# Two-layer transformer kernel on one core: VectorE's share of the softmax exponentials as E + E(1+f)(1+f)/2 from 16-bit patterns

## The chip, the core and the metric

The kernel runs on one core of a Trainium2 chip. TensorE (PE) multiplies matrices into PSUM; its weight loads (PEld) are shown apart. ScalarE (ACT) evaluates functions such as exp, VectorE (DVE) does elementwise work on SBUF and PSUM, GpSimd (POOL) does elementwise work on SBUF alone, and SyncE (SP) issues the DMAs. Each engine takes its instructions in program order and waits on semaphores for the others. The metric is the device time of one launch in microseconds, as the median over repeated runs; lower is better.

## The reference

Two layers with the same weights, 2048 tokens, width 448, 16 heads of 28, hidden width 1792, all in bf16. Each layer is an attention block and an MLP with squared ReLU, both behind a layer norm and with a residual.

```python
def _A_ref(x, wqkv, wo):                      # H = 16, Dh = 28
    qkv = (x @ wqkv).reshape(B, S, 3, H, Dh).transpose(2, 0, 3, 1, 4)
    q, k, v = qkv[0], qkv[1], qkv[2]
    p = softmax(einsum("bhqd,bhkd->bhqk", q, k) * Dh ** -0.5)
    o = einsum("bhqk,bhkd->bhqd", p, v)
    return o.transpose(0, 2, 1, 3).reshape(B, S, D) @ wo
def _B_ref(x, w1, b1, w2, b2):
    h = relu(einsum("bsd,df->bsf", x, w1) + b1)
    return einsum("bsf,fd->bsd", h * h, w2) + b2
x = x + _A_ref(_layernorm(x), A_wqkv, A_wo)
x = x + _B_ref(_layernorm(x), B_w1, B_b1, B_w2, B_b2)
x = x + _A_ref(_layernorm(x), A_wqkv, A_wo)
x = x + _B_ref(_layernorm(x), B_w1, B_b1, B_w2, B_b2)
```

The softmax needs 16 x 2048 x 2048 exponentials in each layer. The kernel takes exp without subtracting the row's maximum, sums the exponentials by extra columns of ones in V, and divides at the end.

## The kernel before

**Units, groups, passes.** The attention of a layer is cut into passes (one query block of 256 or 128 rows, four heads, a range of key blocks) and a pass into units: one head, 512 scores for each of 128 partitions. There are 2048 units. A group takes three units: TensorE writes their transposed scores into the three banks of one PSUM tile `sc` (L1061, four row tiles of 32 so that heads run beside each other), of which there are two. ScalarE then turns a group's scores into bf16 exponentials in an SBUF tile `pt` (L1087), 1536 columns wide if all three units are its own, 1024 wide if the third was given to VectorE. There are 683 groups and twelve `pt` buffers. When enough key blocks of a pass have their exponentials, TensorE multiplies them by V into the pass's PSUM tile `oT` (L1284, four column tiles of 32). Projections, layer norms and the MLP of other query blocks are worked into the same stream (L769 for their matmuls).

**A unit on VectorE.** The queries are scaled so that a score is a power of two in fixed point (`FRAC` = 17 fraction bits). VectorE reads the scores from PSUM, adds a constant and limits them from below (`take`, L1148) into 32-bit integers in one of the rooms `R_v` (`v_y`, or parts of K and V that are free). Their halves are a fraction and an exponent. `line` (L1177) makes a linear function of the fraction in fp16, `power` (L1191) makes a power of two, E, from the exponent as a bf16 pattern; both may run on GpSimd or VectorE. `square` (L1194) squares the line's result on VectorE and `close` (L1200) multiplies it by E. The exponential is E + a·a·E. Where a buffer is free for it, E stays and is multiplied by V on its own, as a second product in the same TensorE operation (`twice`); else `one` (L1197) adds 1 before the closing product. The result stands in the third part of the group's own `pt`, or, if the unit belongs to a later pass, in a cell `R_pd` (tile `pd`, or free parts of V, K, or the hidden tiles).

**The planner.** The order of all instructions is made in Python before the launch. Streams (`s_stream` scores, `e_stream` ScalarE's exponentials, `p_stream` value matmuls, `a_unit`/`a_rest` for units on VectorE, the chains of the MLP) offer their next operation with a cost and the resources that it takes and frees; `Planner.run` takes the one that can start first, with priorities, and holds back a TensorE operation that would make the next scores late. Operations marked `port` on VectorE and GpSimd take turns. `apart` decides whether a group's third unit goes to VectorE: by VectorE's load over the last `SPAN` us against `BUSY` or, when the MLP work is `behind`, against `LOW`, and by its backlog against `TB`/`TB2`. `PACE` holds parameter values that apply from a group's number on; `FORCE` and `SKIP` list groups in which `apart` answers yes or no without asking for the load.

Of the kernel before, what the change touches and what calls it, by code (L numbers as in the profile page):

```python
# [55 lines left out]
L0E = 1280  # L56
L0N = 4.8
L1E = 1900
L1N = 5.6
# [79 lines left out]
FORCE = (17, 47, 84, 107, 111, 144, 215, 237, 240, 241, 271, 322, 341, 347, 354, 363, 368, 379, 404, 413, 423, 428,  # L139
         434, 438, 440, 453, 457, 472, 495, 512, 515, 532, 561, 608, 614, 628, 633, 640, 641, 648, 652, 667)  # L140
SKIP = (20, 38, 46, 66, 190, 202, 227, 235, 246, 299, 302, 357, 362, 384, 461, 465, 474, 475, 489, 504, 520, 542,
        607, 649, 650)
PACE = {
    0: {'BUSY': 1.05, 'LOW': 1.0, 'CHUNK': 2, 'EV': 2.9, 'FAR': 6, 'KEEP': 2, 'L1N': 5.2, 'LAG': 3, 'LEAD': 18,
         'MARGIN': -1, 'MORE': 1, 'PRE': 0.5, 'SLACK': 0.7, 'SPAN': 11, 'TB': 1.6, 'TB2': 0.9, 'V_AGE': 6, 'V_LAST':
         3, 'V_PAST': 2, 'C_PRIO': 1.6, 'V_PRIO': 8.5, 'V_LATE': 3.5, 'V_WAIT': 5, 'EPRIO': 6, 'ASIDE': 2.0,
         'SPARE': 1, 'VSPARE': 2, 'NEAR': 3, 'SOON': 0.3, 'VGAP': 0.03, 'PWAIT': 1, 'PNEAR': 0.2, 'PORTP': 0.0},
    8: {'V_PAST': 5, 'LEAD': 12},
    16: {'SPAN': 8, 'EPRIO': 4, 'SPARE': 3, 'PRE': 0.8},
    24: {'V_AGE': 2},  # L150
    32: {'V_AGE': 8},
    40: {'MORE': 3, 'V_LAST': 2.5},
    48: {'MORE': 1, 'TB2': 3.0},
    56: {'VSPARE': 1},
    64: {'TB': 2.0, 'PNEAR': 0.15, 'MARGIN': 1.5},
    72: {'KEEP': 6},
    88: {'PWAIT': 4, 'TB2': 0.6, 'C_PRIO': 1.2},
    96: {'EV': 1.3},
    104: {'EPRIO': 6, 'V_PAST': 0, 'CHUNK': 3},
    120: {'V_LAST': 3, 'PWAIT': 1, 'SPARE': 1, 'L1N': 5.6},  # L160
    128: {'TB': 4.2},
    136: {'TB': 2.2, 'V_AGE': 3},
    144: {'TB': 1.6, 'V_LAST': 2.2, 'V_LATE': 4.6, 'PWAIT': 4},
    152: {'V_AGE': 5},
    176: {'EV': 2.2},
    184: {'V_LAST': 3, 'SPARE': 0},
    240: {'SPAN': 15, 'LOW': 0.8},
    248: {'V_PAST': 2, 'PORTP': 1},
    272: {'SPARE': 3},
    280: {'MARGIN': -3, 'SPARE': 1},  # L170
    288: {'VGAP': 0, 'NEAR': 9},
    296: {'SPARE': 0, 'SOON': 0.6},
    312: {'V_AGE': 6},
    320: {'PWAIT': 0.6},
# [12 lines left out]
    440: {'V_LATE': 2.6, 'V_LAST': 3},
    456: {'MARGIN': 0.5, 'LOW': 0.9, 'V_PRIO': 4},
    464: {'PRE': 0.5},
    496: {'L1N': 5.0},  # L190
    512: {'VSPARE': 3, 'KEEP': 4, 'V_LAST': 2.2},
    520: {'BUSY': 1.02, 'ASIDE': 0},
    528: {'V_AGE': 5, 'V_WAIT': 2},
    536: {'EV': 1.5, 'VSPARE': 1, 'SPAN': 8},
    552: {'V_AGE': 2, 'C_PRIO': 1.6},
    560: {'V_LAST': 3, 'PORTP': 1},
    608: {'L1N': 5.6},
    616: {'L1N': 5.8, 'LAG': 12, 'V_LATE': 3.5, 'SPARE': 2},
    624: {'VSPARE': 20},
    632: {'ASIDE': 0.5},  # L200
    640: {'SPARE': 3},
    648: {'V_LAST': 2.5},
    664: {'CHUNK': 2, 'L1N': 5.0},
# [29 lines left out]
LAT = {"PE": 0.25, "ACT": 0.3, "DVE": 0.07, "POOL": 0.10, "DMA": 2.0, "-": 0.0}  # L233
# [5 lines left out]
class Planner:  # L239
# [3 lines left out]
    def __init__(self):  # L243
        self.clock = {"PE": 0.0, "ACT": 0.0, "DVE": 0.0, "POOL": 0.0, "DMA": 0.0, "-": 0.0}
# [53 lines left out]
    def run(self):  # L298
        while self.streams:
# [61 lines left out]
            self.clock[e] = o.end - (OVER if e == "DVE" and o.dur > 0.1 else 0.0) + (PGAP if e == "POOL" else 0.0)  # L361
# [22 lines left out]
def kernel(  # L384
# [556 lines left out]

    def apart(i, now, us, soon=SOON):
# [4 lines left out]
        if sum(r.when() is not None and r.when() <= now + soon for r in sets_of(units[i])) <= (0 if soon else pending[0]):  # L947
            return None
# [640 lines left out]
```

## Time and profile before

| | |
|---|---|
| median of 3 runs | 817.91 us (817.5 to 819.25) |
| profiled execution | 821.79 us, of which the span is 817.4 us |
| TensorE clock granted | 0.996 |
| TensorE busy | 783.8 us (96%), 12133 matmuls |
| VectorE busy | 768.5 us (94%), 1784 instructions |
| ScalarE busy | 801.3 us (98%), 700 instructions |
| GpSimd busy | 422.9 us (52%), 678 instructions |
| DMA | 17.99 MB, mean 22 GB/s; 255 GB/s in the first 20 us |

Each row of the page's table of costly groups reads: line of the kernel, engine, operation, output tile <- input tiles, shapes, count | busy time in us, mean ns of one | idle time of the engine just before these instructions, and what ended most of it. Busy time counts overlapping instructions of the group once. Rows of a timeline give the start in us, the duration in us and the count. Rows by stretches give, after the bounds, the busy us of PE, PEld, DVE, ACT and POOL with the number of instructions, the granted clock, and the DMA's share and GB/s.

### The profile page before, as it was taken

Reading aid. Unit: us, or ns where it says so; the run is one execution under the profiler, and the core shown is the slowest. Engines: PE = TensorE matmul, PEld = TensorE weight load, DVE = VectorE, ACT = ScalarE, POOL = GpSimd, SP = SyncE. Lnnn points to the kernel's source line nnn. Section 1 sums busy time; section 2 is a strip of 40 time slices with the busy share of each in tenths; the row PEclk is TensorE's granted clock in tenths of the full one; section 3 lists DMA queues with packets and bytes.
Section 4 is the critical chain, followed back from the end, with each engine's and each line's share of the span. In section 5 each row is a group of like instructions: output and inputs, shape, how many; then the busy total and the mean of one; then the engine's idle time right before and its main releaser. Section 6 shows DMA issues by size and latency. Waiting matters only on the chain.

```text
span 817.4 us, 28983 instructions
## 1 busy us (share of the span) xinstructions
PE 783.8 (96%) x12133; PEld 427.8 (52%) x12133; DVE 768.5 (94%) x1784; ACT 801.3 (98%) x700; POOL 422.9 (52%) x678
## 2 busy tenths in 40 slices
PE   8999999999999999999999999879999999999998
PEld 4555554554554555555455545445454545545666
DVE  8999999999999999999999999999999999999954
ACT  8999999999999999999999999999999999999994
POOL 3356756566556466554555566665556455412400
PEclk9999999999999999999999999989999999999999
DMA  9200010000000000000000000011000000000000
GB/s 255 73 3 2 15 28 18 16 17 16 16 3 15 16 16 16 15 4 15 2 2 3 2 3 2 16 29 29 24 20 21 21 27 15 28 14 15 22 14 13
DMA packets 32318, 17.99 MB, mean 22 GB/s; under 512 B 17786, under 2 KB 31739, under 8 KB 32188
## 3 DMA queue, kind: packets, MB, share of 16 engines
q1 hardware_dynamic: 32188, 16.16, 7.1%
q8 instruction: 94, 1.54, 0.8%
q14 instruction: 36, 0.29, 0.1%
HBM read 13.87 MB, written 2.06 MB: 19 GB/s over the span
## 4 chain that ended last, share of the span: by engine, by line
PE 69%; ACT 16%; DVE 10%; issue 3%; DMA 1%; POOL 0%; ACTq 0%; SPq 0%; DVEq 0%
PE mt L769 29%; PE sc L1061 22%; PE oT L1284 16%; ACT pt L1087 16%; PE tp L672 2%; DVE v_y L1148 1%; DVE r L1480 1%; DVE st L619 1%; DVE pt L1200 1%; PE sc L769 1%; DVE K_sb L1148 1%; DVE K_sb L792 1%; DMA rec<-scr 1%; DVE pt L1194 1%; DVE xn L732 0%
## 5 line engine op out<-in xcount | busy, mean ns | idle before, releaser
L1087 ACT ACTIVATE pt<-sc 128x1536 bf16<-128x1536 f32 (+1 forms) x683 | 789.8, 1337 | 3.9 <-PE sc L1061 3.4
L1061 PE MATMUL sc<-Q_sb,K_sb 32*128 32x256 bf16 (+1 forms) x4712 | 283.0, 266 | 27.7 <-ACT pt L1087 24.4
L1061 PEld LDWEIGHTS <-K_sb 32*128 32x128 bf16 x4712 | 103.1, 92 | 199.8 <-issue 135.7
L1284 PEld LDWEIGHTS <-V_sb 128*32 128x32 bf16 x4922 | 127.9, 96 | 47.4 <-issue 40.6
L1284 PE MATMUL oT<-pt,V_sb 128*32 128x256 bf16 (+1 forms) x4196 | 151.6, 269 | 0.0
L1177 POOL TENSOR_SCALAR pt<-v_y 128x512 f16<-128x512 uint16 x121 | 78.5, 648 | 98.9 <-DVE v_y L1148 29.7
L769 PE MATMUL mt<-xnT,w 128*128 128x256 bf16 (+1 forms) x896 | 118.7, 271 | 0.0
L1148 DVE TENSOR_SCALAR v_y<-sc 128x512 int32<-128x512 f32 x163 | 110.5, 680 | 2.4 <-PE sc L1061 1.8
L1194 DVE TENSOR_TENSOR pt<-pt 128x512 f16<-128x512 f16 x234 | 96.4, 423 | 3.4 <-POOL pt L1177 3.3
L769 PEld LDWEIGHTS <-w 128*128 128x128 bf16 x952 | 78.0, 98 | 34.4 <-issue 26.2
L1480 DVE TENSOR_SCALAR r<-mt 128x512 bf16<-128x512 f32 x108 | 73.1, 677 | 2.1 <-PE mt L769 1.7
L769 PE MATMUL mt<-w,V_sb 128*128 128x448 bf16 (+1 forms) x288 | 68.9, 348 | 0.0
L1191 POOL TENSOR_SCALAR v_y<-v_y 128x512 int16<-128x512 int16 x70 | 45.5, 650 | 30.6 <-DVE pt L1194 9.3
L1148 DVE TENSOR_SCALAR K_sb<-sc 128x512 int32<-128x512 f32 x81 | 55.0, 680 | 1.6 <-PE sc L1061 1.4
L1177 POOL TENSOR_SCALAR pt<-K_sb 128x512 f16<-128x512 uint16 x56 | 36.4, 651 | 33.9 <-DVE K_sb L1148 15.0
L1420 DVE TENSOR_TENSOR x_sb<-x_sb,mt 128x448 bf16<-128x448 bf16 (+1 forms) x62 | 37.5, 604 | 9.4 <-PE mt L769 9.0
L1177 POOL TENSOR_SCALAR pt<-V_sb 128x512 f16<-128x512 uint16 x45 | 30.2, 671 | 24.3 <-DVE V_sb L1148 7.8
L1148 DVE TENSOR_SCALAR V_sb<-sc 128x512 int32<-128x512 f32 x61 | 41.5, 680 | 1.2 <-PE sc L1061 0.9
L1200 DVE TENSOR_TENSOR pt<-pt,K_sb 128x512 bf16<-128x512 f16 x92 | 39.8, 433 | 0.3
L619 DVE BATCH_NORM_STATS2 st<-x_sb 128x6 f32<-128x448 bf16 x62 | 37.9, 613 | 0.7 <-DMA x_sb<-in_A_x_dram 0.4
L769 PEld LDWEIGHTS <-V_sb 128*128 128x128 bf16 x302 | 24.9, 98 | 25.0 <-issue 11.2
L1284 PE MATMUL oT<-K_sb,V_sb 128*32 128x256 bf16 x214 | 34.1, 274 | 0.0
(157 smaller groups left out, 1048.9 us busy)
## 6 DMA issues: line engine op xcount, KB each, us to landing
rec<-scr SPq DMA_DIRECT2D x54, 128.0 KB
x_sb<-in_A_x_dram SPq DMA_DIRECT2D x8, 224.0 KB
out_dram<-x_sb SPq DMA_DIRECT2D x15, 112.0 KB
w<-in_B_w_dram SPq DMA_DIRECT2D x1, 1568.0 KB
w<-in_B_w_dram SPq DMA_DIRECT2D x1, 1344.0 KB
dn<-oT_sb SPq DMA_DIRECT2D x54, 4.0 KB
V_sb<-in_A_wqkv_dram SPq DMA_DIRECT2D x4, 168.0 KB
scr<-dn SPq DMA_DIRECT2D x27, 8.0 KB
```

The source lines that it names most:

```text
L619: nc.vector.bn_stats(out=box["st"][:, :], in_=x_sb[:, t0 + j, :] if src is None else src())
L769: nc.tensor.matmul(box["t"][:, c0:c0 + n], lhsT=lhsT() if callable(lhsT) else lhsT, rhs=rhs, start=a, stop=b)
L1061: nc.tensor.matmul(dst[k][:, i * nt * P:(i + 1) * nt * P], lhsT=K_sb[l][rows, g, (kb + i) * P:(kb + i + 1) * P], rhs=Q_sb[rows, g, t0 * P: ...
L1087: t = nc.scalar.activation(out=pt[:, 0:n], in_=gbuf[gi]["sc"][:, 0:n], func=AF.Exp, scale=float(np.log(2.0)) * 2.0 ** -FRAC)
L1148: t = nc.vector.tensor_scalar(out=y, in0=src, scalar1=EXP_BIAS, scalar2=EXP_LOW, op0=ALU.add, op1=ALU.max)
L1177: on(e).tensor_scalar(out=box["a"], in0=box["f"], scalar1=EXP_LINE[0], scalar2=EXP_LINE[1], op0=ALU.add, op1=ALU.mult)
L1191: on(e).tensor_scalar(out=box["e"].bitcast(DT.int16), in0=box["n"], scalar1=64.0, scalar2=EXP_BASE, op0=ALU.mult, op1=ALU.add)
L1194: nc.vector.tensor_tensor(out=box["a"], in0=box["a"], in1=box["a"], op=ALU.mult)
L1200: nc.vector.tensor_tensor(out=box["pd"], in0=box["aa"], in1=box["e"], op=ALU.mult)
L1284: nc.tensor.matmul(box["t"][DHP * hh:DHP * hh + DHP, 0:n], lhsT=V_sb[l][:, tb, 4 * g + hh, :], rhs=p, start=begin and j < G, stop=close an ...
L1420: nc.vector.tensor_tensor(out=x_sb[:, tb, lo:hi], in0=x_sb[:, tb, lo:hi], in1=t[:, 0:hi - lo], op=ALU.add)
L1480: nc.vector.tensor_scalar(out=r[:, 0:w], in0=t[:, 0:w], scalar1=0.0, scalar2=None, op0=ALU.max)
```

## The change

A score now has 7 fraction bits, so that adding a constant and rounding to a 16-bit integer gives the pattern of a bf16 number z = E(1+f), E a power of two and f the fraction of the mantissa. A unit on VectorE takes these steps, with line numbers of the changed kernel:

- `take` (L1124): scores from PSUM plus a constant, limited from below, as int16 patterns z. They go straight into the third part of the group's `pt`, or into a cell for a later pass.
- `whole` (L1146): E. On GpSimd, z - 63.5 + 1.5·2^30, which rounds to whole powers of two and leaves E's pattern in the low half of each 32-bit word, in a room `R_v`. On VectorE it would be a mask; the order has all 309 on GpSimd.
- `half` (L1150): mask and set of bits on VectorE, which give (1+f)/2 as bf16, in a cell.
- `close` (L1154): z times that, in place: E(1+f)(1+f)/2.

The exponential is E + E(1+f)(1+f)/2, of which E is always a product with V of its own. These products are TensorE operations of their own (L1221), collected over heads (`XMIN`), between the pass's other value matmuls (L1257). A new stream `t_stream` takes the `pt` buffer when the scores are there, since VectorE may be the first to write it. `room_for` and `cell_for` keep some rooms and cells for the oldest pass. `apart` asks for free cells rather than rooms and prefers a head that has had few such units. `behind` compares with a table of progress (`TRACK`). `FORCE` and `SKIP` become empty, and of the parameter table only the set at group 0 remains, with other values.

```diff
-FRAC = 17
-EXP_BIAS = -0.03899196872583688 * 2.0 ** FRAC
-EXP_LOW = -56.0 * 2.0 ** FRAC
-EXP_BASE = 126.0 * 2.0 ** 7 + 27.0
-EXP_LINE = (2.40163417 * 2.0 ** 16, 0.34787667 * 2.0 ** -16)
+FRAC = 7
+EXP_MEAN = 0.58627
+EXP_BASE = (127.0 - EXP_MEAN) * 2.0 ** FRAC
+WHOLE = 1.5 * 2.0 ** 30
+EXP_LOW = 160.0
...
+ADUR = 0.29
+LADD = 0.15
+HDUR = 0.30
+RES = 2
+RES2 = 4
+XMIN = 4
...
-FORCE = (17, 47, 84, 107, 111, 144, 215, 237, 240, 241, 271, 322, 341, 347, 354, 363, 368, 379, 404, 413, 423, 428,
...
-SKIP = (20, 38, 46, 66, 190, 202, 227, 235, 246, 299, 302, 357, 362, 384, 461, 465, 474, 475, 489, 504, 520, 542,
...
+FORCE = ()
+SKIP = ()
 PACE = {
-    0: {'BUSY': 1.05, 'LOW': 1.0, 'CHUNK': 2, 'EV': 2.9, 'FAR': 6, 'KEEP': 2, 'L1N': 5.2, 'LAG': 3, 'LEAD': 18,
...
-    8: {'V_PAST': 5, 'LEAD': 12},
-    16: {'SPAN': 8, 'EPRIO': 4, 'SPARE': 3, 'PRE': 0.8},
...
+    0: {'BUSY': 1.0, 'LOW': 0.8, 'CHUNK': 2, 'EV': 2.9, 'FAR': 6, 'KEEP': 2, 'LAG': 3, 'LEAD': 18, 'MARGIN':
+        6, 'MORE': 1, 'PRE': 0.5, 'SLACK': 0.7, 'SPAN': 20, 'TB': 1.6, 'TB2': 1, 'V_AGE': 8, 'V_LAST': 3,
+        'V_PAST': 2, 'C_PRIO': 2.6, 'V_PRIO': 4.5, 'V_LATE': 3.5, 'V_WAIT': 5, 'ASIDE': 1, 'SPARE': 3, 'NEAR':
+        3, 'SOON': 0.3, 'VGAP': 0.03, 'PWAIT': 1, 'PNEAR': 0.2, 'PORTP': 0.0, 'HOLD': 5, 'XMIN': 2, 'LADD':
+        0.05, 'RES2': 2},
 }
...
-        return done[l] < (min(i, b) - a) / (b - a) * n * per[l] - MARGIN
+        return done[l] < np.interp(i, *TRACK[l]) - MARGIN
...
+    def room_for(unit):
+
+        c = sets_of(unit)
+        if sum(r.when() is not None for r in c) <= (RES2 if unit[0] > p_now[0] else 0):
+            return ()
+        old = min((pi for pi, n in open_adds.items() if n), default=unit[0])
+        if old < unit[0] and sum(r.when() is not None for r in sets_of((old, *unit[1:]))) <= RES:
+            return ()
+        return c
+
+    def cell_for(unit):
+
+        c = pd_free(unit)
+        return c if sum(r.when() is not None for r in c) > pending[0] else ()
...
+        heads = by_head.get(units[j][0], {})
+        j = min(js, key=lambda k: (heads.get(units[k][3], 0), k)) if js else j
...
+            o = gbuf[gi]["t"] = Op("+", 0.0, fn, deps=[("s", gi)], acq=R_pt, need=n + own, sets=("t", gi))
...
-            t = nc.vector.tensor_scalar(out=y, in0=src, scalar1=EXP_BIAS, scalar2=EXP_LOW, op0=ALU.add, op1=ALU.max)
+            z = gbuf[gi]["z"] = gbuf[gi]["pt"][:, 1024:1536] if own else pd_of(c)
+            t = nc.vector.tensor_scalar(out=z.bitcast(DT.int16), in0=src, scalar1=EXP_BASE, scalar2=EXP_LOW, op0=ALU.add, op1=ALU.max)
...
+        def whole(e):
+            z = gbuf[gi]["z"].bitcast(DT.int16)
+            y = room_of(w.res, l)
+            if e == "DVE":
+                gbuf[gi]["e2"] = y.bitcast(DT.bfloat16)[:, 0:512]
+                nc.vector.tensor_scalar(out=gbuf[gi]["e2"].bitcast(DT.int16), in0=z, scalar1=0x7F80, scalar2=None, op0=ALU.bitwise_and)
...
+                gbuf[gi]["e2"] = y.bitcast(DT.bfloat16).rearrange("p (n t) -> p n t", t=2)[:, :, 0]
+                nc.gpsimd.tensor_scalar(out=y, in0=z, scalar1=-63.5, scalar2=WHOLE, op0=ALU.add, op1=ALU.add)
+
+        def half(e):
+            box["f"] = pd_of(h)
+            nc.vector.tensor_scalar(out=box["f"].bitcast(DT.int16), in0=gbuf[gi]["z"].bitcast(DT.int16), scalar1=0x7F, scalar2=0x3F00,
+                                    op0=ALU.bitwise_and, op1=ALU.bitwise_or)
 
         def close(e):
-            nc.vector.tensor_tensor(out=box["pd"], in0=box["aa"], in1=box["e"], op=ALU.mult)
...
+            nc.vector.tensor_tensor(out=gbuf[gi]["z"], in0=gbuf[gi]["z"], in1=box["f"], op=ALU.mult)
+        w = Op(("POOL", "DVE"), (EDUR, ADUR), whole, deps=[c], acq=lambda: room_for(unit), sets=("w", gi), port=True)
...
+        h = Op("DVE", HDUR, half, deps=[c], acq=lambda: cell_for(unit), port=True)
...
+        o = Op("DVE", 0.42, close, deps=[h, w], rel=h, sets=("x", gi), port=True)
...
+                begin = "o" not in box
+                if not begin and batch and (len(batch) >= XMIN or final):
+                    batch = list(batch.values())
+                    more = [m for m in more if m not in batch]
+
+                    def fn(e, batch=batch, box=box, l=l, g=g, r=r, n=n):
+                        for i in range(r):
+                            for gi, hh, kb in batch:
+                                nc.tensor.matmul(box["t"][DHP * hh:DHP * hh + DHP, 0:n], lhsT=V_sb[l][:, kb + i, 4 * g + hh, :],
+                                                 rhs=gbuf[gi]["e2"][:, i * n:(i + 1) * n], start=False, stop=False,
+                                                 tile_position=(0, DHP * hh))
+                    yield Op("PE", 0.23, fn, deps=[("w", gi) for gi, *_ in batch], rel=[pl.tok["w", gi] for gi, *_ in batch], mode="col")
+                    continue
```

More of the change, by code (lines that the diff above doesn't have):

```diff
@@ L230, in __init__ @@
         self.need, self.got, self.more, self.port, self.soft = need, [], 0.0, port, False
-LAT = {"PE": 0.25, "ACT": 0.3, "DVE": 0.07, "POOL": 0.10, "DMA": 2.0, "-": 0.0}
+LAT = {"PE": 0.25, "ACT": 0.3, "DVE": 0.07, "POOL": 0.10, "DMA": 2.0, "-": 0.0, "+": 0.0}
 USE = {"row": 0.7, "col": 0.98, "full": 0.93}
@@ L243, in __init__ @@
     def __init__(self):
-        self.clock = {"PE": 0.0, "ACT": 0.0, "DVE": 0.0, "POOL": 0.0, "DMA": 0.0, "-": 0.0}
+        self.clock = {"PE": 0.0, "ACT": 0.0, "DVE": 0.0, "POOL": 0.0, "DMA": 0.0, "-": 0.0, "+": 0.0}
         self.mode = None
@@ L360, in run @@
             o.end += o.more
[L361 removed]
+            self.clock[e] = 0.0 if e == "+" else o.end - (OVER if e == "DVE" and o.dur > 0.1 else 0.0) + (PGAP if e == "POOL" else 0.0)
             if e == "ACT" and o.dur > 0.1:
@@ L1267, in fn @@
                         box["t"] = bank(box["o"], "oT")
-                    held[0] -= sum(k == 3 and (not gbuf[gi]["in"]) + ("h" in gbuf[gi]) for kb in now for gi, k, _ in where[pi, kb])
+                    held[0] -= sum(k == 3 and not gbuf[gi]["in"] for kb in now for gi, k, _ in where[pi, kb])
                     todo = []
```

227 lines of the change are left out of this document (73 added, 154 removed).

## The prediction

> **What bounds the kernel now.** I read the page's busy line first, then ScalarE's timeline at both ends, then the busy time by stretches.
>
> ```profile
> span 817.4 us, 28983 instructions
> PE 783.8 (96%) x12133; PEld 427.8 (52%) x12133; DVE 768.5 (94%) x1784; ACT 801.3 (98%) x700; POOL 422.9 (52%) x678
> L1087 ACT ACTIVATE pt<-sc 128x1536 bf16<-128x1536 f32 (+1 forms) x683 | 789.8, 1337 | 3.9 <-PE sc L1061 3.4
> ...
> 9.57 1.44 ACT L1087 ACTIVATE pt<-sc 128x1536 bf16<-128x1536 f32 x1
> 160.19 4.70 ACT L1087 ACTIVATE pt<-sc 128x1024 bf16<-128x1024 f32 x5
> 779.32 23.95 ACT L1087 ACTIVATE pt<-sc 128x1536 bf16<-128x1536 f32 x18
> ...
> 300.00:400.00 100.00, 97.65 (x1428) 51.61 (x1427) 95.74 (x219) 100.00 (x87) 55.46 (x90) 1.00 0.04 10
> 500.00:600.00 100.00, 89.80 (x1389) 48.03 (x1382) 94.91 (x216) 98.02 (x87) 60.92 (x95) 0.97 0.09 24
> 600.00:700.00 100.00, 97.52 (x1503) 51.51 (x1503) 99.78 (x235) 99.95 (x90) 54.91 (x83) 1.00 0.07 19
> 780.00:817.40 37.40, 33.50 (x693) 22.62 (x687) 17.00 (x45) 26.98 (x25) 1.30 (x3) 1.00 0.05 14
> ```
>
> In the stretch rows the columns are PE, PEld, DVE, ACT, POOL. ScalarE does one exponential after another from 9.57 us to 803.27 us (779.32 + 23.95), 683 of them: 793.7 us, of which 3.9 idle. In front of it stand 9.6 us of loading and first projections, behind it 14.1 us (the last normalisation, projection and MLP), and 4.4 us between the span and the profiled execution's 821.79 us. So the time is 28.1 us plus the exponentials. VectorE is nearly full beside it (up to 99.78 of 100 us), GpSimd half.
>
> Of ScalarE's 3.9 us idle, 3.4 are waits for scores. But the idle column understates what is lost, because one exponential begins before the last has ended. Two rows above give the undisturbed pitch. Eighteen wide ones take 23.95 us, and the form rows give the length of one:
>
> ```profile
> L1087 ACT ACTIVATE pt<-sc 128x1536 bf16<-128x1536 f32 x377 | 546.1, 1528 | 2.5 <-PE sc L1061 2.1
> L1087 ACT ACTIVATE pt<-sc 128x1024 bf16<-128x1024 f32 x306 | 321.9, 1102 | 1.4 <-PE sc L1061 1.3
> ```
>
> With 546.1/377 = 1.45 for the last, the other seventeen have (23.95 - 1.45)/17 = 1.324 us each; five narrow ones in 4.70 us with 321.9/306 = 1.05 for the last give (4.70 - 1.05)/4 = 0.912. Then 377 x 1.324 + 306 x 0.912 = 778.2 us is what the exponentials need, and 793.7 - 778.3 (with the last one's overhang) = **15.4 us is lost** to late scores, mostly in pieces too short to be seen as idle. That loss is what the change can really move.
>
> **The change, part by part.** Counts for the changed kernel come from its instruction order, which is known though it hasn't run.
>
> *ScalarE.* There are 309 key-block units on VectorE instead of 305, so four groups lose 512 columns: 373 wide and 310 narrow. 4 x (1.324 - 0.912) = **-1.6 us**. Three MLP halves at the end stay on it instead of seven short instructions; they sit behind the last exponential among PE waits. Head and tail I leave at 9.6 and 14.1: the opening is the same code, and though 24 fewer MLP matmuls stand behind the last score matmul, these were filler beside the normalisation chain.
>
> *VectorE and GpSimd.*
>
> ```profile
> L1148 DVE TENSOR_SCALAR v_y<-sc 128x512 int32<-128x512 f32 x163 | 110.5, 680 | 2.4 <-PE sc L1061 1.8
> L1194 DVE TENSOR_TENSOR pt<-pt 128x512 f16<-128x512 f16 x234 | 96.4, 423 | 3.4 <-POOL pt L1177 3.3
> L1200 DVE TENSOR_TENSOR pt<-pt,K_sb 128x512 bf16<-128x512 f16 x92 | 39.8, 433 | 0.3
> L1177 DVE TENSOR_SCALAR pt<-v_y 128x512 f16<-128x512 uint16 x7 | 2.9, 413 | 0.0
> L1177 POOL TENSOR_SCALAR pt<-v_y 128x512 f16<-128x512 uint16 x121 | 78.5, 648 | 98.9 <-DVE v_y L1148 29.7 <-ACT pt L1087 14.5 <-DVE pt L1200 9.1
> L1191 POOL TENSOR_SCALAR v_y<-v_y 128x512 int16<-128x512 int16 x70 | 45.5, 650 | 30.6 <-DVE pt L1194 9.3 <-DVE pt L1177 2.8 <-DVE V_sb L1487 2.8
> L732 DVE TENSOR_SCALAR xn<-x_sb,mv,rstd 128x448 bf16<-128x448 bf16 x64 | 25.1, 409 | 2.3 <-POOL rstd L650 2.0
> L619 DVE BATCH_NORM_STATS2 st<-x_sb 128x6 f32<-128x448 bf16 x62 | 37.9, 613 | 0.7 <-DMA x_sb<-in_A_x_dram 0.4
> ...
> L1197 DVE TENSOR_SCALAR pt<-pt x10: 277/283/587, 366.1 to 765.9; 128x512 f16<-128x512 f16 x10
> ...
> 15.95 1.04 DVE st L619 x2
> ```
>
> Two statistics in a row took 1.04 us, 0.52 each against a mean of 0.613, so an instruction holds VectorE for 0.09 less than its duration. Removed: 305 squares x (0.423 - 0.09) = 101.6; 20 additions of one x 0.19 = 3.8; 26 line and power steps that ran on VectorE x (0.413 - 0.09) = 8.4. Added: 309 mask-and-or instructions, for which the trace has no row. Bounds: at best the 16-bit add of a constant, L1197 at 0.283; the two-operation tensor-scalar L732 at 0.409; at worst the 0.680 of L1148. The new one has L1197's shape, 512 contiguous 16-bit values in place of SBUF, so I take 0.283 and keep the others for the range: 309 x 0.193 = 59.6. Four more units add 4 x (0.59 + 0.34) = 3.7. Sum: -113.8 + 63.3 = **-50 us, 768.5 to about 718**. On GpSimd 584 instructions of 0.65 us go (-380) and 309 roundings come: from the 0.65 of the two POOL rows (they read and write no more than it, so I see no gain) to 1.3, double, were the int32 output that much dearer; the rows nearest to it say 0.65, so +201, and 423 becomes about 244. Both lie beside ScalarE's exponentials, so neither 50 nor 180 us comes off the time: their worth is only in a smaller loss. A VectorE unit now has two steps behind the rounding instead of up to four, and the pairs of GpSimd passes in a row are gone.
>
> The 261 new waits of VectorE's first step on ScalarE point at an exponential eight to thirteen groups back, ten microseconds old: 0.
>
> *TensorE.*
>
> ```profile
> L1061 PE MATMUL sc<-Q_sb,K_sb 32*128 32x256 bf16 (+1 forms) x4712 | 283.0, 266 | 27.7 <-ACT pt L1087 24.4 <-DVE oTn L1411 0.5 <-DVE Q_sb L788 0.4
> L1284 PEld LDWEIGHTS <-V_sb 128*32 128x32 bf16 x4922 | 127.9, 96 | 47.4 <-issue 40.6 <-DVE xn L732 0.4 <-DVE xnT L684 0.4
> ...
> 779.95 0.33 PE sc L1061 x12
> 782.98 1.01 PE oT L1284 x64
> 809.55 0.89 PE mt L769 x16
> ```
>
> Value matmuls go from 4922 to 4986 (4352 as before plus 634 for E; before 570 were second products), score matmuls from 4712 to 4780, of 256 columns mostly. TensorE's free 27.7 us before scores are nearly all waits for ScalarE, so its total is no bound. What counts is the order: a score group stands behind whatever TensorE was given since the last one, and if that is longer than one exponential, ScalarE starves. From the chain rows I price 128 columns at 0.0275 us for a score matmul (0.33/12), 0.0158 for a value matmul (1.01/64) and 0.0556 for a full one (0.89/16), add up the work between successive score groups in both orders, and set it against the exponentials' 1.324 and 0.912. Stretches above their exponential: 168 before, 206 after, by 56.7 and 63.8 us in all; pairs of stretches above their pair: 140 and 175, by 43.2 and 51.9; triples 89 and 123, by 30.0 and 37.3. So TensorE's feed is **12 to 25% more uneven** in the new order. This comes with the part of the change that the name leaves out: the table that set the planner's parameters group by group, and 67 forced or skipped groups, give way to one set for the whole run. Besides, E's 634 matmuls form operations of their own, and 300 of them begin with a wait for GpSimd (before, 230 value matmuls waited for it and 196 for VectorE; now 186 for VectorE). Behind such a wait stand the next score groups, and behind those ScalarE. A rounding that lands late by a few tenths therefore costs what one late score costs.
>
> Taking the triples' 24% for the loss, 15.4 becomes 19.1, and I add 1 us for 60 more waits in TensorE's queue at about 0.02 each (15.4 us over 683 groups is 0.023): **loss 20 us, +4.6**. Bounds: 8 (half of the present loss, since VectorE is looser) and 34 (the present one doubled).
>
> *Sum.* 821.8 - 1.6 + 4.6 = 824.8 us in the profiled execution's own terms. That execution was 3.9 us above the median of its three runs (817.91), so I forecast a median of **821 us**.
>
> **One rule against the change.** One of the ten L1197 adds took 0.587 us, twice its median. The Trainium skill, Advanced Engine Details and Errata, section VectorE Performance Modes, says that a two-port VectorE instruction and GpSimd block each other at the shared SBUF port; the changed kernel has 309 instead of 20 of these. By that rule, if no turns were kept, the mask would cost 0.587 and the third rival below would hold; by the nine other adds it costs 0.283 and the sum stands. The planner gives each of the two engines turns at the port, before and after.
>
> **The rivals.**
>
> 1. *The freed VectorE time pays.* VectorE's work between the takes of four successive units exceeds ScalarE's in 76 cases in the new order against 125, by 35 against 56 us (durations from the rows above). If late VectorE steps, and not TensorE's queue, make most of the loss, it falls to 5-13 us: 821.8 - 1.6 - 6.4 = 813.8, less 3.9: **810** with 9 lost. For it: 99.78 of 100 us busy at 600-700. Against it: ScalarE's 3.4 us of seen waits end on score matmuls, and that stretch lost no more than others (ACT 99.95).
> 2. *Nothing moves.* The freed time isn't spent (four more units only), and the loss stays at 15.4: 821.8 - 1.6 - 3.9 = **816.3**, at the very edge of what can be told.
> 3. *VectorE becomes the bound.* Place: the mask step. At 0.587 it adds 309 x 0.30 = 94 us, 718 becomes 812; VectorE is without work for some 30 us of head and tail (20.4 of 37.4 in the last row above alone), so the span is at least 842, and the median 842 + 4.4 - 3.9 = **843**. It decides from about 0.50 (718 + 309 x 0.22 = 786, plus 30). At 0.409 VectorE would be at 757, about where it is now. A GpSimd rounding of 1.3 us ends alike: the closing product waits for it, and 244 us become 445.
>
> **How the numbers follow.** Forecast, loss 17.5 to 31: 0.42. Rival 2, loss 13.5 to 17.5 (814.4 to 818.4): 0.21. Rival 1: 0.25. Rival 3, or a loss above 31: 0.12. A measurement of this kernel tells about 0.2% (1.6 us) from no change, so same is 816.3 to 819.5. Faster: rival 1 and half of rival 2, 0.35. Same: the other half and the low edge of the forecast, 0.15. Slower: 0.50. The range 808 to 837 leaves out one in ten on either side: below it a loss under 7, above it a loss over 36 or a full VectorE. The forecast's own range is 818.5 to 832.
>
> **What would show it.** Exponentials: 373 and 310, first at 9.6 us, and 793.7 - 1.6 + 4.6 = 796.7 us from first to last. The mask near 0.28, VectorE near 718 us busy, the rounding near 0.65 and GpSimd near 244. ScalarE's waits for score matmuls longer than 3.4 us, with E matmuls or MLP matmuls in front of the late scores. I am wrong if the exponentials take under 792 us, if the mask takes 0.4 or more, or if the tail differs from 14.1 us by over 2.

## The result, and the profile after

| | before | changed |
|---|---|---|
| median | 818.58 us (817.5 to 820.19, 4 runs) | 961.24 us (960.29 to 963.74, 4 runs) |
| ratio, 95% interval | | 1.1746 (1.1714 to 1.1777) |
| profiled execution, its span | 821.79, 817.4 us | 963.74, 961.8 us |

Slower, as forecast, but by 143 us instead of 3, and, as the runs below show, in the main for another reason. The profile's page of the changed kernel, with the busy times, the shares of the chain that ended last, and the groups that matter:

```profile
span 961.8 us, 29126 instructions
PE 829.8 (86%) x12271; PEld 426.9 (44%) x12271; DVE 764.3 (79%) x1754; ACT 820.9 (85%) x696; POOL 664.8 (69%) x403
...
POOL 35%; PE 27%; DVE 26%; issue 10%; ACT 1%; POOLq 0%; DVEq 0%; ACTq 0%
...
L1068 ACT ACTIVATE pt<-sc 128x1536 bf16<-128x1536 f32 (+1 forms) x683 | 811.2, 1268 | 127.3 <-PE sc L1030 97.4
L1146 POOL TENSOR_SCALAR v_y<-pt 128x512 int32<-128x512 int16 x155 | 313.2, 2021 | 100.3 <-DVE pt L1124 75.2
L1154 DVE TENSOR_TENSOR pt<-pt,V_sb 128x512 bf16<-128x512 bf16 x85 | 37.6, 443 | 41.0 <-POOL v_y L1146 21.6
```

No engine is full any more: the busiest is at 86%. The chain, which in the kernel before ran through GpSimd for 0% of the span, runs through it for 35%. The rounding takes 2.02 us; 0.65 was put into the sum. ScalarE's idle time is 127.3 us, 97.4 of them for late scores. Its timeline at both ends:

```profile
9.71 1.45 ACT L1068 ACTIVATE pt<-sc 128x1536 bf16<-128x1536 f32 x1 [0.62 <-PE sc L1030]
...
912.49 35.13 ACT L1068 ACTIVATE pt<-sc 128x1536 bf16<-128x1536 f32 x26 [0.42 <-PE sc L1030]
```

The exponentials run from 9.71 to 947.62 us: 937.9 us where 796.7 were predicted. Head (9.7) and tail (961.8 - 947.62 = 14.2) did not change. The whole loss lies among the exponentials, and it is spread over the run; two stretches (busy us of PE, PEld, DVE, ACT, POOL, then the granted clock) have ScalarE at 87 of 100 us, and VectorE too far from full:

```profile
300.00:400.00 100.00, 85.23 (x1273) 43.98 (x1272) 83.33 (x189) 87.44 (x76) 79.90 (x48) 1.00 0.04 10
600.00:700.00 100.00, 84.17 (x1219) 39.84 (x1214) 78.87 (x185) 86.88 (x75) 77.33 (x43) 0.91 0.09 24
```

A stretch of the timeline shows how a late rounding gets there (start, duration, line, and in brackets the idle time ahead and what ended it):

```profile
243.91 4.40 POOL L1146 TENSOR_SCALAR V_sb<-K_sb 128x512 int32<-128x512 int16 x2
...
246.11 0.42 DVE L1154 TENSOR_TENSOR K_sb<-K_sb 128x512 bf16<-128x512 bf16 x1 [1.01 <-POOL V_sb L1146]
...
246.45 0.70 DVE L1150 TENSOR_SCALAR pd<-K_sb 128x512 int16<-128x512 int16 x1
...
248.35 0.43 DVE L1154 TENSOR_TENSOR K_sb<-K_sb,pd 128x512 bf16<-128x512 bf16 x1 [1.20 <-POOL V_sb L1146]
248.69 0.68 DVE L1124 TENSOR_SCALAR pt<-sc 128x512 int16<-128x512 f32 x1
...
249.43 0.61 PE L1030 MATMUL sc<-Q_sb,K_sb 32*128 32x256 bf16 x6 [2.44 <-DVE pt L1124]
...
250.14 1.45 ACT L1068 ACTIVATE pt<-sc 128x1536 bf16<-128x1536 f32 x1 [2.24 <-issue]
```

Two roundings in a row fill 4.40 us. VectorE's two closing products stand still behind them, for 1.01 and 1.20 us. The next `take` stands behind these in VectorE's order and reads its scores late, so the score bank comes free late, TensorE waits 2.44 us for it, and ScalarE stands for 2.24 us. The profile names nothing that ended this last wait (`issue`); the scores that the exponential reads end just before it, at 250.04. Over the whole run VectorE's closing products wait 114.9 us for GpSimd (the three rows of what ended idle time before line L1154):

```profile
  POOL v_y L1146: 61.0, 73
  POOL K_sb L1146: 34.3, 39
  POOL V_sb L1146: 19.6, 22
```

### The profile page after: what moved, and what is told of

Its sections match the earlier page's. It is cut to its first block, busy times and chain, and to the rows that moved or that the text cites. A ratio compares the mean times of both kernels' runs of the same rounds, so it can differ in the third digit from the quotient of the medians.

```text
span 961.8 us, 29126 instructions
## 1 busy us (share of the span) xinstructions
PE 829.8 (86%) x12271; PEld 426.9 (44%) x12271; DVE 764.3 (79%) x1754; ACT 820.9 (85%) x696; POOL 664.8 (69%) x403
## 4 chain that ended last, share of the span: by engine, by line
POOL 35%; PE 27%; DVE 26%; issue 10%; ACT 1%; POOLq 0%; DVEq 0%; ACTq 0%
POOL v_y L1146 17%; PE mt L717 13%; POOL K_sb L1146 9%; POOL V_sb L1146 8%; PE sc L1030 8%; DVE pt L1124 8%; PE oT L1257 4%; DVE r L1450 3%; DVE pt L1154 2%; PE oT L1221 1%; ACT pt L1068 1%; DVE st L567 1%; DVE xn L680 1%; DVE x_sb L1390 1%; POOL rstd L598 1%
## 5 line engine op out<-in xcount | busy, mean ns | idle before, releaser
L1068 ACT ACTIVATE pt<-sc 128x1536 bf16<-128x1536 f32 (+1 forms) x683 | 811.2, 1268 | 127.3 <-PE sc L1030 97.4
L1146 POOL TENSOR_SCALAR v_y<-pt 128x512 int32<-128x512 int16 x155 | 313.2, 2021 | 100.3 <-DVE pt L1124 75.2
L1030 PE MATMUL sc<-Q_sb,K_sb 32*128 32x256 bf16 (+1 forms) x4780 | 291.0, 272 | 54.4 <-DVE pt L1124 37.2
L1030 PEld LDWEIGHTS <-K_sb 32*128 32x128 bf16 x4780 | 102.0, 93 | 239.7 <-issue 131.4
L1124 DVE TENSOR_SCALAR pt<-sc 128x512 int16<-128x512 f32 x269 | 181.6, 681 | 24.1 <-PE sc L1030 22.4
L1257 PE MATMUL oT<-pt,V_sb 128*32 128x256 bf16 (+1 forms) x4270 | 177.3, 275 | 9.9 <-DVE pt L1154 6.8
L1146 POOL TENSOR_SCALAR K_sb<-pt 128x512 int32<-128x512 int16 x68 | 139.4, 2049 | 62.4 <-DVE pt L1124 43.5
L1257 PEld LDWEIGHTS <-V_sb 128*32 128x32 bf16 x4352 | 100.6, 97 | 65.5 <-issue 60.6
L1146 POOL TENSOR_SCALAR V_sb<-pt 128x512 int32<-128x512 int16 x46 | 91.8, 1995 | 28.3 <-DVE pt L1124 19.8
L1450 DVE TENSOR_SCALAR r<-mt 128x512 bf16<-128x512 f32 (+1 forms) x109 | 74.2, 681 | 7.4 <-PE mt L717 7.2
L1154 DVE TENSOR_TENSOR pt<-pt,V_sb 128x512 bf16<-128x512 bf16 x85 | 37.6, 443 | 41.0 <-POOL v_y L1146 21.6
L717 PE MATMUL mt<-w,V_sb 128*128 128x448 bf16 (+2 forms) x288 | 69.7, 352 | 0.0
L1221 PE MATMUL oT<-v_y,V_sb 128*32 128x256 bf16 (+1 forms) x348 | 45.1, 280 | 17.3 <-POOL v_y L1146 17.1
L1154 DVE TENSOR_TENSOR pt<-pt,K_sb 128x512 bf16<-128x512 bf16 x79 | 34.4, 442 | 19.0 <-POOL v_y L1146 10.2
L1221 PEld LDWEIGHTS <-V_sb 128*32 128x32 bf16 x634 | 26.2, 97 | 50.8 <-issue 49.3
L1154 DVE TENSOR_TENSOR pt<-pt,pd 128x512 bf16<-128x512 bf16 x64 | 28.5, 446 | 25.4 <-POOL v_y L1146 17.6
L1390 DVE TENSOR_TENSOR x_sb<-x_sb,mt 128x448 bf16<-128x448 bf16 (+2 forms) x62 | 37.3, 604 | 5.6 <-PE mt L717 5.6
L597 POOL TENSOR_TENSOR ve<-mv,eps_t 128x2 f32<-128x2 f32 (+1 forms) x33 | 8.9, 269 | 44.3 <-DVE mv L572 39.7
```

The lines of the kernel that those rows point to most:

```text
L717: nc.tensor.matmul(box["t"][:, c0:c0 + n], lhsT=lhsT() if callable(lhsT) else lhsT, rhs=rhs, start=a, stop=b)
L1030: nc.tensor.matmul(dst[k][:, i * nt * P:(i + 1) * nt * P], lhsT=K_sb[l][rows, g, (kb + i) * P:(kb + i + 1) * P], rhs=Q_sb[rows, g, t0 * P: ...
L1068: t = nc.scalar.activation(out=pt[:, 0:n], in_=gbuf[gi]["sc"][:, 0:n], func=AF.Exp, scale=float(np.log(2.0)) * 2.0 ** -FRAC)
L1124: t = nc.vector.tensor_scalar(out=z.bitcast(DT.int16), in0=src, scalar1=EXP_BASE, scalar2=EXP_LOW, op0=ALU.add, op1=ALU.max)
L1146: nc.gpsimd.tensor_scalar(out=y, in0=z, scalar1=-63.5, scalar2=WHOLE, op0=ALU.add, op1=ALU.add)
L1154: nc.vector.tensor_tensor(out=gbuf[gi]["z"], in0=gbuf[gi]["z"], in1=box["f"], op=ALU.mult)
```

## The experiments

Ratios are to the kernel before, in runs on the same chip, with 95% intervals.

### Why the rounding takes 2 us

**e1: another type written.**

```diff
-                nc.gpsimd.tensor_scalar(out=y, in0=z, scalar1=-63.5, scalar2=WHOLE, op0=ALU.add, op1=ALU.add)
+                nc.gpsimd.tensor_scalar(out=y.bitcast(DT.float32), in0=z, scalar1=-63.5, scalar2=WHOLE, op0=ALU.add, op1=ALU.add)
```

> The changed kernel, with one thing different: the GpSimd rounding writes fp32 words instead of int32 words to the same place, in the same order of instructions. E's pattern is then not what the value matmuls need, so the values of E are wrong; all the work is there. Theory A (the rounding is slow because its result is int32; everything else of the change runs as planned): the rounding falls from 2.0 us to 0.65 to 0.8, GpSimd's busy time from 665 to about 250 us, ScalarE's idle time before exponentials from 127 to under 15 us, and the time from 961 to 815-830 us. Theory B (512 four-byte results cost 2.0 us on GpSimd whatever their type): rounding 2.0 us, time 955-965. Theory C (the new order and the E matmuls of their own starve ScalarE as well): rounding 0.65 us, but the time stays above 850.

959.65 us, ratio 1.1712 (1.1677 to 1.1746), and the rounding still takes 1.92 us at least. So it is not the conversion to integers, the one thing that the prediction had named for a dearer rounding.

**e4 and e5: the instruction by itself.** Two kernels that hold nothing but rows of such instructions, with types and widths varied in e4, and the pair of operations in e5:

```diff
+    run("wff", DT.float32, f, 512)
+    run("wssadd", DT.int16, z, 512, s1=1.0, s2=2.0)
+    run("wsimul", DT.int32, z, 512, s1=0.0078125, s2=-0.5, op0=ALU.mult, op1=ALU.add)
...
+    A, S, M, X, N = ALU.add, ALU.subtract, ALU.mult, ALU.max, ALU.min
+    pair("pAA", A, A)
+    pair("pMA", M, A, s1=1.0)
+    pair("pMS", M, S, s1=1.0, s2=-WHOLE)
```

> No transformer: only six of each of a row of tensor-scalar instructions of 128 partitions on GpSimd, with input and output types, widths and constants varied, and three kinds on VectorE; the output is zeros. Theory A (int32 as the output type is what is slow): int16 to int32 2.0 us at 512 columns, also with small constants and from fp32; int16 to fp32, to int16 and to bf16 0.65 us or little more. Theory B (four-byte output): int16 to fp32 and fp32 to fp32 near 2.0 as well. Theory C (the large constant): int16 to int32 with small constants 0.65. On VectorE the two-operation mask 0.28 us, as in the changed kernel.

The groups of e4 by line and form:

```profile
L44 POOL TENSOR_SCALAR wff<-f 128x512 f32<-128x512 f32 x6 | 11.5, 1921 | 0.5
...
L44 POOL TENSOR_SCALAR wssadd<-z 128x512 int16<-128x512 int16 x6 | 11.5, 1921 | 0.0
...
L44 POOL TENSOR_SCALAR wsimul<-z 128x512 int32<-128x512 int16 x6 | 3.7, 618 | 0.0
```

> No transformer: four each of GpSimd tensor-scalar instructions, 128x512, int16 to int32, that differ only in their pair of operations; the output is zeros. In the first probe add-add took 1.92 us with every type and with small constants, multiply-add 0.62. Theory A (only the pair add-add lacks the fast path): subtract-add, add-subtract, add-multiply, multiply-multiply all near 0.62. Theory B (any pair without a multiplication is slow): every pair of add, subtract, max and min 1.9, every pair with a multiplication 0.62. A single add or multiplication 0.62 under both.

The groups of e5:

```profile
L44 POOL TENSOR_SCALAR pAA<-z 128x512 int32<-128x512 int16 x4 | 7.7, 1929 | 1.8 <-DVE z L34 1.6
...
L44 POOL TENSOR_SCALAR pMS<-z 128x512 int32<-128x512 int16 x4 | 7.7, 1923 | 0.0
...
L64 POOL TENSOR_SCALAR pA<-z 128x512 int32<-128x512 int16 x4 | 6.0, 1497 | 0.3
L67 POOL TENSOR_SCALAR pMul<-z 128x512 int32<-128x512 int16 x4 | 6.0, 1488 | 0.2
...
L44 POOL TENSOR_SCALAR pMM<-z 128x512 int32<-128x512 int16 x4 | 2.5, 618 | 0.0
L44 POOL TENSOR_SCALAR pMA<-z 128x512 int32<-128x512 int16 x4 | 2.5, 617 | 0.1
L44 POOL TENSOR_SCALAR pAM<-z 128x512 int32<-128x512 int16 x4 | 2.5, 617 | 0.1
```

With the one pair add-add, the time is 1.92 us for every type tried, in and out; only the row of the first instructions, int16 to int32, has a mean of 2.44, with single ones up to 4.79 while VectorE is at work too, and its later ones take 1.92 as well. With one type, it is 0.62 us for three pairs (mult-mult, mult-add, add-mult), 1.92 to 1.93 for the other ten tried, and 1.49 to 1.50 for a single operation. Two theories fall in part: a multiplication doesn't make it fast (mult-subtract and subtract-mult are slow), and a single operation isn't at 0.62 either. The two GpSimd steps of the kernel before are add-mult (L1177) and mult-add (L1191), two of the three fast pairs; the new rounding is add-add.

**e12: the other direction.** The kernel before, with the constant's sign turned in `power` and the same values computed:

```diff
-            on(e).tensor_scalar(out=box["e"].bitcast(DT.int16), in0=box["n"], scalar1=64.0, scalar2=EXP_BASE, op0=ALU.mult, op1=ALU.add)
+            on(e).tensor_scalar(out=box["e"].bitcast(DT.int16), in0=box["n"], scalar1=64.0, scalar2=-EXP_BASE, op0=ALU.mult, op1=ALU.subtract)
```

> The kernel before with one thing changed: the step power (L1191, mult 64 and add a constant) subtracts the negated constant instead, the pair mult-subtract, which took 1.92 us by itself; values, types, order and waits stay the same. 296 of them are on GpSimd: 423 + 296 x 1.27 = about 800 us of GpSimd. Theory 'the pair of operations alone, whatever the kernel': power takes 1.92 to 2.05 us and the time rises to 900 to 1000 us, with VectorE's closing product waiting for GpSimd. Theory 'the length comes from the changed kernel's own surroundings' (tiles, rooms, its order): power stays under 1 us and the time near 819.

1033.31 us, ratio 1.2606 (1.2560 to 1.2652), above the expected 900 to 1000. Its groups on GpSimd:

```profile
L1191 POOL TENSOR_SCALAR v_y<-v_y 128x512 int16<-128x512 int16 x70 | 142.4, 2034 | 11.9 <-DVE pt L1194 2.3 <-DVE rq L1359 1.1 <-DVE x_sb L1420 0.8
L1177 POOL TENSOR_SCALAR pt<-v_y 128x512 f16<-128x512 uint16 x121 | 87.7, 725 | 32.1 <-DVE v_y L1148 9.9 <-DVE xnT L684 6.4 <-PE mt L769 3.7
```

`power` goes from 0.65 to 2.03 us, while add-mult at L1177 beside it goes only from 0.65 to 0.73. So the length belongs to the pair of operations, in either kernel.

### What the plan is worth with the rounding that it assumed

**e6 and e7: the same order with a shorter rounding.** E is rounded to the nearest power of two here. First e6, then e7:

```diff
-                nc.gpsimd.tensor_scalar(out=y, in0=z, scalar1=-63.5, scalar2=WHOLE, op0=ALU.add, op1=ALU.add)
+                nc.gpsimd.tensor_scalar(out=y, in0=z, scalar1=1.0, scalar2=WHOLE, op0=ALU.mult, op1=ALU.add)
```

```diff
-                nc.gpsimd.tensor_scalar(out=y, in0=z, scalar1=-63.5, scalar2=WHOLE, op0=ALU.add, op1=ALU.add)
+                nc.gpsimd.tensor_scalar(out=y, in0=z, scalar1=WHOLE, scalar2=None, op0=ALU.add)
```

> The rounding's pair of operations add-add becomes mult-add (times 1, plus 1.5 x 2^30); types, widths, order and waits stay as in the changed kernel. E is then rounded to the nearest power of two, so values differ for about half of the elements. Theory 'the pair alone': the rounding takes 0.62 to 0.65 us, GpSimd is busy about 244 us, VectorE waits under 10 us for it, and the prediction's sum holds: about 821 us, within 808 to 837, ScalarE idle under 15 us. Theory 'the order too': the more uneven feed of TensorE and the E matmuls standing in front of score groups cost much by themselves, and the time stays above 845 us although the rounding is short.

825.18 us (822.96 to 826.31, 5 runs), ratio 1.0073 (1.0049 to 1.0097). The page of e6, then its timeline of ScalarE:

```profile
PE 784.0 (95%) x12271; PEld 419.7 (51%) x12271; DVE 741.0 (90%) x1754; ACT 800.4 (97%) x696; POOL 245.3 (30%) x403
...
L1146 POOL TENSOR_SCALAR v_y<-pt 128x512 int32<-128x512 int16 x155 | 104.7, 676 | 230.8 <-DVE pt L1124 157.4
```

```profile
9.44 1.45 ACT L1068 ACTIVATE pt<-sc 128x1536 bf16<-128x1536 f32 x1 [0.28 <-PE sc L1030]
...
774.16 33.37 ACT L1068 ACTIVATE pt<-sc 128x1536 bf16<-128x1536 f32 x25
```

One pair of operations makes 136 of the 143 us. What is left is near the change as it was predicted: GpSimd 245.3 us, exponentials from 9.44 to 807.53, 798.1 us. With 373 x 1.324 + 310 x 0.912 + 0.1 = 776.7 needed, 21.4 are lost (15.4 before).

> The rounding becomes one addition, which took 1.50 us by itself (between 0.62 and 1.92); order and waits as in the changed kernel; E is rounded to the nearest power of two. Theory 'each rounding is waited for': the loss grows with the rounding's length in proportion, from the time with 0.62 to 961 us with 1.92 to 2.02, so 1.50 gives 64 to 68% of the way: about 910 to 920 us. Theory 'a threshold': the time stays near the short rounding's until GpSimd is full or a backlog forms; then 1.50 gives under 870 us.

873.7 us (2 runs), ratio 1.0662 (1.0633 to 1.0692), between the two theories: 36% of the way. Its rounding has a mean of 1.55 us. From 0.68 to 1.55 us a longer rounding costs (873.7 - 825.2) / 0.87 = 56 us for each us, from 1.55 to 2.03 us (961.2 - 873.7) / 0.48 = 182. With 309 roundings that is 0.18 and then 0.59 of each one's added length.

### Which wait costs what

**e8, e9, e10: the rounding stays at 2 us, and one wait or both are taken away.** The first edit is e8's, the second e9's, and e10 has both.

```diff
-                                                 rhs=gbuf[gi]["e2"][:, i * n:(i + 1) * n], start=False, stop=False,
+                                                 rhs=w1[:, 0, i * n:(i + 1) * n], start=False, stop=False,
```

```diff
-            nc.vector.tensor_tensor(out=gbuf[gi]["z"], in0=gbuf[gi]["z"], in1=box["f"], op=ALU.mult)
+            nc.vector.tensor_tensor(out=box["f"], in0=gbuf[gi]["z"], in1=box["f"], op=ALU.mult)
```

> The E matmuls read a constant tile instead of E, so TensorE waits for no rounding any more; VectorE's closing product still does. Leaves out E's product with V. Theory 'through VectorE' (GpSimd late -> closing product late -> the next takes late -> the PSUM tile free late -> scores late -> ScalarE): under 10% of the 143 us come off, so above 945 us, and VectorE still waits over 50 us for GpSimd. Theory 'through TensorE' (the prediction's: behind an E matmul's wait stand the score groups): over half comes off, under 890 us.

947.22 us: 14.0 us come off, a tenth, and VectorE's closing products still wait 115.2 us for GpSimd (114.9 in the changed kernel).

> The closing product writes into the cell of the mask's result instead of over z, so it waits no more for the rounding that reads z; the value matmuls read z itself, so E(1+f)(1+f)/2 is left out of the sum. TensorE's E matmuls still wait for the rounding, which still takes 2 us. Theory 'through VectorE': over half of the 143 us come off, under 890 us, and the takes are on time (VectorE idle before L1124 falls). Theory 'through TensorE': above 930 us, with TensorE idle in front of L1221 grown well above 17 us.

891.07 us: 70.2 us come off, 49% of the 143, a little short of "over half". The closing product doesn't wait any more, TensorE's waits in front of L1221 stay as they were (15.9 us in the largest row, 17.1 before that edit). What TensorE and its weight loads wait for takes (of what ended idle time before line L1030, in the changed kernel, in e8 and in e9) shows the way through VectorE:

```profile
  DVE pt L1124: 109.5, 158
```

```profile
  DVE pt L1124: 142.6, 175
```

```profile
  DVE pt L1124: 24.4, 61
```

One expected sign failed: VectorE's idle time before its takes did not fall but rose, from 25.7 to 57.0 us of waits for scores. VectorE now stands ready for the scores; before, it came late to them. The edit also takes away a smaller wait, since the value matmuls (L1257) no longer need the closing product: TensorE waited 6.8 us for it in the changed kernel and nothing in e9, so not quite all of the 70.2 us is VectorE's wait.

> Both edits at once: the E matmuls read a constant tile and the closing product writes into the mask's cell, so neither TensorE nor VectorE's closing product waits for a rounding, which still takes 2 us on GpSimd. Leaves out E's product with V and E(1+f)(1+f)/2. Waits that stay: a rounding for its take, and takes and masks that write over tiles which an older rounding reads. Theory 'the two waits are all': the time of the short rounding comes back, 825 us, at most 835. Theory 'the rounding harms in itself' (the SBUF port held beside VectorE, tiles kept for longer): about as with one wait gone, 870 us or more; between the two it is shared.

860.55 us: 100.7 us come off, and 35 us over e6 remain, though neither of the two waits is left and no take, mask or closing product waits for GpSimd in this trace. One wait for GpSimd has grown. This kernel's row, then the same row of e6 (us in all, times, the longest):

```profile
DVE xn L680 <- POOL rstd L598: 23.9, 16, 6.9
```

```profile
DVE xn L680 <- POOL rstd L598: 3.8, 8, 0.9
```

The third way: the layer norm has two small steps on GpSimd (L597, L598), and they queue behind the roundings. The timeline of e10, GpSimd, VectorE, TensorE and ScalarE:

```profile
200.38 5.92 POOL L1146 TENSOR_SCALAR v_y<-pt 128x512 int32<-128x512 int16 x3
206.38 0.20 POOL L597 TENSOR_TENSOR ve<-mv,eps_t 128x2 f32<-128x2 f32 x1
206.65 0.71 POOL L598 TENSOR_TENSOR rstd<-ve,mhalf 128x2 f32<-128x2 f32 x1
...
207.39 0.70 DVE L680 TENSOR_SCALAR xn<-x_sb,mv,rstd 128x448 bf16<-128x448 bf16 x2 [6.90 <-POOL rstd L598]
...
207.84 1.03 PE L620 MATMUL tp<-ident,xn 128*128 128x128 bf16 x8 [5.03 <-DVE xn L680]
...
209.53 1.45 ACT L1068 ACTIVATE pt<-sc 128x1536 bf16<-128x1536 f32 x1 [5.52 <-PE sc L1030]
```

Set side by side from the first exponential on, e10 falls 38.6 us behind e6; 34.3 of these arise in 226 of the 682 steps from one exponential to the next, those with a start of a normalisation (L680) at most 7 us before the step or 2 us after its end, and 4.3 in the other 456. That places the rest; no run took the normalisation off GpSimd to confirm it.

### Three ways to compute the same values

**e2, e3, e11.** e2: the planner is told 1.98 us for the rounding, and puts E on VectorE as a mask where that is better. e3: E is always a mask on VectorE. e11: two fast GpSimd passes, planned at 1.30 us together. In this order:

```diff
-EDUR = 0.617
+EDUR = 1.98
```

```diff
-        w = Op(("POOL", "DVE"), (EDUR, ADUR), whole, deps=[c], acq=lambda: room_for(unit), sets=("w", gi), port=True)
+        w = Op("DVE", ADUR, whole, deps=[c], acq=lambda: room_for(unit), sets=("w", gi), port=True)
```

```diff
-                nc.gpsimd.tensor_scalar(out=y, in0=z, scalar1=-63.5, scalar2=WHOLE, op0=ALU.add, op1=ALU.add)
+                nc.gpsimd.tensor_scalar(out=gbuf[gi]["e2"].bitcast(DT.int16), in0=z, scalar1=-63.5, scalar2=2.0 ** -7, op0=ALU.add, op1=ALU.mult)
+                nc.gpsimd.tensor_scalar(out=gbuf[gi]["e2"].bitcast(DT.int16), in0=gbuf[gi]["e2"].bitcast(DT.int16), scalar1=128.0, scalar2=0.0, op0=ALU.mult, op1=ALU.add)
```

> The changed kernel, planned with 1.98 us instead of 0.617 us for the rounding on GpSimd. The planner now puts 169 of 281 roundings on VectorE as a mask (planned at 0.29 us) and 112 on GpSimd. Theory A (the cost is that the plan took the rounding for three times shorter than it is, so VectorE and TensorE stand in order behind results that come late): with the same slow instruction but a true plan the loss mostly goes; 28 units fewer on VectorE cost 28 x 0.41 = 11.5 us on ScalarE, so 825-845 us. Theory B (GpSimd's long occupation of the port that it shares with VectorE is itself the cost, planned or not): 112 x 2.0 us still block VectorE, and the time stays above 870.

> The changed kernel with all E steps as masks on VectorE, none on GpSimd; 291 units instead of 309. VectorE gains 291 x 0.19 = 55 us and loses 18 units x 1.2 us. Theory A (the GpSimd rounding is the whole of the slowdown): ScalarE needs 18 x 0.41 = 7.4 us more than in the changed kernel, and the time is 820-835 us. Theory B (the rest of the change starves ScalarE too): above 850 us.

> E exact on GpSimd in two passes of the pairs that took 0.62 us: add -63.5, times 2^-7 to an int16 exponent, then times 128, add 0. Its order is made for 1.30 us for both; 274 units on VectorE instead of 309. ScalarE's work is 35 x (1.324 - 0.912) = 14.4 us above the changed kernel's. Theory 'the pair alone': each pass takes 0.62 to 0.68 us, the loss on ScalarE stays as with the short rounding, 825 + 14.4 = about 840 us, 832 if the smaller number of units lowers the loss. Theory 'each rounding is waited for, and 1.3 us are too long for this scheme': above 855 us, like the single addition.

| | narrow exponentials | median | ratio (95%) | VectorE, GpSimd busy |
|---|---|---|---|---|
| e2 | 282 | 841.11 us | 1.0268 (1.0241 to 1.0296) | 722.8, 260.0 us |
| e3 | 292 | 834.68 us | 1.0212 (1.0157 to 1.0267) | 752.9, 37.1 us |
| e11 | 275 | 844.67 us | 1.0308 (1.0281 to 1.0334) | 720.5, 396.4 us |

All three undo most of the loss, and none beats the kernel before, nor e6. One of e3's four runs took 843.1 us, the others 833.7 to 835.5; its profile, and so the busy times in the table, are of the longest. In e2, 112 roundings of 2 us do no such harm: the order is made for them, and the rest are masks; which of the two does it was not separated. e11's passes take 0.68 and 0.63 us, 1.32 in all, in an order made for that; VectorE's closing products wait 1.3 us for GpSimd in the whole run, so the single addition's loss doesn't return, though 844.67 is 4.7 us above the 840 expected. Each gives VectorE fewer units than the changed kernel with its 310 narrow exponentials, and each unit less is 0.41 us more of ScalarE.

## Why the prediction was right and wrong

**The step that failed** is one line of the VectorE and GpSimd term: "from the 0.65 of the two POOL rows ... to 1.3, double, were the int32 output that much dearer; the rows nearest to it say 0.65, so +201". The rounding took 2.02 us, and GpSimd 664.8 instead of 244. The rows were chosen by engine, shape and width, and the bound by the output's type; what sets the duration is the pair of operations (e5, e6, e12), and in that the rows were no neighbours: they are add-mult and mult-add. The Trainium skill, GPSIMD Engine Reference, section Elementwise — side-by-side cycle accounting, gives 769 ns as measured for 512 elements in a tight loop, with no figure for a pair of operations; 0.62 us here is under it and 1.92 far over it.

The sum also had no price for a rounding that comes late while VectorE has time left: rival 3 priced it by a full VectorE, and the forecast gave 1 us to all added waits in TensorE's queue. Taking away the closing products' wait, and with it a small wait of TensorE's, brought 70 of the 143 us back (e9). That the change is slower was forecast from TensorE's uneven feed, so the right direction of the 143 us is luck; e6 is the run that tests the forecast's own reason.

**The rest of the sum was close.** With a rounding of 0.68 us (e6): 825.18 us measured against 821 forecast; exponentials 798.1 us against 796.7; a loss of 21.4 us against 20; 373 and 310 exponentials; head and tail 9.4 and 14.2. The added time is 6.5 us on the same chip (818.67 before), about twice the 3 forecast. That the more uneven feed of TensorE makes it fits the price of 4.6 us for a loss that grew by 6.0, but no run shows it: ScalarE's seen waits for scores are 3.6 us against 3.4, and masks and closing products are longer too.

**The mask** was right where nothing shares the port: 0.28 us (median 283 ns, longest 293, for the commonest forms in e3, where GpSimd is busy 37 us). Beside a working GpSimd the mean of all 309 was 0.323 us in e6 and 0.382 in the changed kernel, single ones up to 0.74. In e4, beside GpSimd instructions without a pause, the mean of twelve was 0.376, where 0.28 had been expected. The row of the changed kernel (count, shortest, median, longest):

```profile
L1150 DVE TENSOR_SCALAR V_sb<-pt x85: 239/288/739, 43.8 to 909.0; 128x512 int16<-128x512 int16 x85
```

That is the contention that the prediction quoted from the Trainium skill, Advanced Engine Details and Errata, section VectorE Performance Modes. The runs agree in part: masks beside a working GpSimd are longer, but none took more than 0.75 us, so none was held for a whole rounding of 2 us. Its part in the loss seems small: it is 309 x (0.382 - 0.283) = 31 us of VectorE's time, and in e10, where the mean is 0.366, the steps away from normalisations lost 4.3 us. No run took the port away by itself.

**VectorE's total** was too low, 718 against 741.0 in e6 and 764.3 in the changed kernel. Counted without overlaps, e6's masks hold VectorE for 75.2 us, where the sum had 59.6, and its closing products for 120.6, where it had 112.1 + 1.4; these are 23 us, and smaller differences on both sides cancel. VectorE still didn't become the bound: it is at 90% in e6.

**The rivals.** Rival 1 (the freed VectorE time pays, 810) and 2 (816.3) fall with e6: VectorE has 27 us less work than before, and the time is 0.5 to 1.0% longer. Rival 3 had the mechanism in its last sentence, the closing product that waits for a long rounding, but made it a matter of VectorE becoming full, with a rounding of 1.3 us and an end at 843. It works by latency: VectorE is at 79% and stands still. The forecast's own words on E matmuls ("behind such a wait stand the next score groups") hold, for 14 us alone and 30.5 once VectorE's wait is gone (891.07 - 860.55).

**What would have shown it** was listed in part. Of the values expected, GpSimd near 244, the rounding near 0.65, VectorE near 718, the mask near 0.28 (0.382 on average, though 0.286 in the median) and exponentials of 796.7 us failed, while the counts, the head and the tail held. But none of the three conditions of "I am wrong if" came true: they asked for exponentials under 792 us and set no upper limit, and neither the rounding nor GpSimd was among them.

## What to carry to other kernels

For GpSimd the nearest row is one with the same two operations; if the trace has none, measure the instruction by itself before planning around it, or write it as a product and a sum. An engine at half load still sets the time if another engine's queue stands behind its result: its latency counts, not its busy time, and small steps of another chain in its own queue wait as well. When a large change costs far more than planned, shorten the one suspect instruction in the same order: that splits what the order costs from what the instruction costs.

## What the runs showed of the hardware

- GpSimd's tensor-scalar on 128x512: 0.617 us for mult-mult, mult-add and add-mult; 1.92 for add-add, mult-subtract and every other pair tried; 1.49 for one operation alone, so a second one that changes nothing (times 1) makes it 2.4 times faster. With add-add, none of the types tried (int16 and fp32 in; int32, fp32, int16 and bf16 out) changed the 1.92.
- On VectorE add-add isn't slow: 0.534 us on average from int16 to int32, 0.36 to 0.82 beside GpSimd's work (e4).
- TensorE's granted clock was lower in some of the stretches in which it was kept waiting: between 600 and 700 us it was 1.00 in e6 (99.31 us busy), 0.91 in the changed kernel (84.17) and 0.80 in e12 (73.19); between 300 and 400 us the changed kernel had 1.00 at 85.23. The Trainium skill, TensorE: Matmul & The Clock Gate, Part 1, ties the clock to how busy TensorE has been lately, which agrees with the first three and not with the last. How much of the added time comes from it wasn't separated.
